# Casts, weight loads, late q rows and the order of the first layer-1 units in a fused attention and MLP kernel

## The chip, the core and the metric

The kernel runs on one core of a Trainium2 chip. The metric is the device time of one execution in microseconds (us), the median of three runs. The engines are TensorE (PE; its weight loads are listed as PEld), VectorE (DVE), ScalarE (ACT), GpSimd (POOL) and SyncE (SP, which here only issues transfers). Transfers issued by SyncE run in the hardware queue q1, those issued by GpSimd in the software queue q0; 16 DMA engines serve both.

## What is computed

Eight batches of eight heads, 576 rows and 64 columns. q is softmaxed over its columns, k over the sequence; kv = kᵀv for each head, and the head's output is q times kv. The heads' outputs side by side are x, 4608 rows by 512, and a two-layer MLP follows with a leaky ReLU between its layers.

```python
def _attn_ref(q, k, v):
    q_s = exp(q - max(q, axis=-1));  q_s = q_s / sum(q_s, axis=-1)
    k_s = exp(k - max(k, axis=2));   k_s = k_s / sum(k_s, axis=2)
    kv = einsum('bhsd,bhse->bhde', k_s, v)
    return einsum('bhsd,bhde->bhse', q_s, kv)

def _moe_ref(x, w_in, w_out):        # 512 x 2048 and 2048 x 512
    h = x @ w_in
    return maximum(0.01 * h, h) @ w_out
```

## The kernel before

**Tiles.** A batch's q, k and v are loaded as tiles of 128 partitions by 4 by 9 by 64: partitions hold two heads' 64 row groups, the 4 is a pair of heads (`HL`), and the 9 (`R`) are sequence rows. Rows are taken in groups: `RA` is rows 0 to 3, `R1` rows 4 and 5, `R2` rows 6 to 8. Head pairs 0 and 1 of a tile (`H0`) and 2 and 3 (`H1`) are also called group `gg` 0 and 1. The MLP works in nine blocks of 512 rows of x (`TT`); block 0 needs most of batch 0, block t most of batch t. x is kept transposed in `xT`, four channel blocks `cb` 0 to 3 by 4608 columns.

**A unit of layer 1** is a pair of output blocks j, j+1 of 128 channels of the 2048. In block 0 the 512 columns are done in two halves of 256. `layer1` (L455) accumulates the four channel blocks in the order 0, 2, 1, 3 into `ph`, a bank of PSUM; `leaky` (L464, ScalarE) evacuates it to `gj`. After half one and half two, 8 units each, `layer2` (L476) accumulates into `pout`: for each j of 16 four matmuls of 512 columns, with `w_out` row block j.

**Before block 0** the code is written out by hand, and each engine runs its own instructions in the order of that text. k's maximum over the sequence goes through TensorE and VectorE (`k_tree` L162, `k_max_pe`, `k_all_dve`, `k_all_pe`), VectorE subtracts it (`k_sub_ps`, L364), ScalarE exponentiates (`k_exp`, L203) and casts v to bf16 with a column of ones behind it (`v_cast`, L213 on ScalarE, L215 elsewhere). `kv_pair` (L293) makes kᵀv and the sums for a group, `kd_rec` and `kd_one` (L375, L379) divide by the sums. q's rows 0 to 3 are exponentiated row by row with their sums (`q_first`, L239), divided (`q_first_rec` L251, `q_norm` L280), transposed on TensorE (`q_transpose`, L392) and copied to `qT` (`q_keep`, L407 on ScalarE, L409 on VectorE). `attend` (L415) multiplies kd with qT and copies the result to `xT` (L425 ScalarE, L427 VectorE). `wake(n)` (L326) puts n dummy matmuls of 512 columns on TensorE. Block 0 starts with four units of half one on channel blocks 0 and 2 only; then `attend` of blocks 1 and 3; then these units are ended with channel blocks 1 and 3.

**Late rows and the next batch** are hung into block 0 by `at(t, u, ...)`: the functions run behind unit step u of block t (half one is 0 to 15, half two 16 to 31, layer 2's j is 32 to 47). `q_max` (L226), `q_sub` (L256), `q_exp` (L264), `q_sum` (L273, L275) and `q_norm` treat R1 and R2; batch 1's k and q preparation hangs on step 15, its exponentials and casts on 29 to 33, its kv on 41, its attends on 46 and 47.

**Loads.** `load` (L79) issues q, k and v on SyncE. `load_w_in(fh)` (L133) issues half fh of w_in (1024 of 2048 output channels) on GpSimd as four transfers, each a quarter: `gg` 0 (channel blocks 0 and 2) in two, `gg` 1 (blocks 1 and 3) in two. `load_w_out(js)` (L140) issues row blocks js. Both cast from f32 to bf16 on the way. A copy of one element into `gate` on GpSimd makes the issues behind it wait: half 0 of w_in for batch 0's k (L513), half 1 for k's subtraction (L539), w_out for the first half of batch 1's k (L569). `hold_sync` (L508) is a small transfer that makes SyncE's later loads wait: batch 1's loads for the first quarter of w_in's half 1, batch 2's for w_out's block 11.

Of the kernel before, what the change touches and what calls it, by code (L numbers as in the profile page):

```python
# [8 lines left out]
FP32 = mybir.dt.float32  # L9
BF16 = mybir.dt.bfloat16  # L10
AF = mybir.ActivationFunctionType
ALU = mybir.AluOpType
# [13 lines left out]
def kernel(  # L26
# [60 lines left out]
    R1, R2 = slice(4, 6), slice(6, R)  # L87
# [38 lines left out]
    w_in_r = moe_w_in.rearrange("(gg hp hh d) f -> gg hp d hh f", gg=2, hp=2, hh=2)  # L126
    w_in_t = w_in_sb.rearrange("p (hh gg) f -> p gg hh f", gg=2)
# [100 lines left out]
    def q_first(b, rs):  # L228
# [3 lines left out]
        qsum = small_pool.tile([P, n, HL], FP32, name="qsum")  # L232
        for hs in (slice(0, 2), slice(2, 4)):
# [3 lines left out]
            for h in range(hs.start, hs.stop):  # L237
                for r in range(n):
                    nc.scalar.activation(  # L239
                        out=st[b]["qe"][:, rs.start + r, h],  # L240
                        in_=st[b]["q"][:, h, rs.start + r],
                        func=AF.Exp,
                        bias=nmax[:, h, r : r + 1],
                        accum_out=qsum[:, r, h : h + 1],
                    )
        st[b]["qsum"] = qsum

    def q_first_rec(b, rs):
        n = rs.stop - rs.start
        st[b]["qrec", rs.start] = qrec = small_pool.tile([P, n, HL], FP32, name="qrec")  # L250
        nc.vector.reciprocal(out=qrec, in_=st[b]["qsum"])  # L251
# [25 lines left out]
    def q_norm(b, rs):  # L277
        n = rs.stop - rs.start
        qes = st[b]["qe"][:, rs]
        nc.vector.tensor_tensor(  # L280
# [245 lines left out]
    k_tree(0, H1, slice(1, 4))  # L526
    k_max_pe(0, 1)
# [17 lines left out]
    wake(4)  # L545
    q_transpose(0, 0, 4)
    kv_pair(0, 1)
    for hh in range(2):
        kd_rec(0, 0, hh)
        kd_one(nc.vector, 0, 0, hh)  # L550
    q_keep(nc.scalar, 0, 0, 4, slice(0, 4, 2))
    q_keep(nc.vector, 0, 0, 4, slice(1, 4, 2))
    attend(0, [0, 2], 0, 256, nc.scalar)
    wake(3)
    kd_rec(0, 1, 0)
    kd_rec(0, 1, 1)
    kd_one(nc.vector, 0, 1, 0)
    kd_one(nc.vector, 0, 1, 1)
    q_max(0, R1)
    q_sub(nc.gpsimd, 0, R1)  # L560
    q_max(0, R2)
# [7 lines left out]
    nc.gpsimd.tensor_copy(out=gate[:, 0:1], in_=st[1]["k"][:, 0, 0, 0:1])  # L569
    for j0, j1 in ((0, 2), (2, 4), (4, 8), (8, 12), (12, 16)):  # L570
        load_w_out(slice(j0, j1))
    hold_sync(1, w_out_sb[0:1, 11, 0:128])
    load_all(2)
# [4 lines left out]
    at(0, 11, lambda: q_transpose(0, 4, 2), lambda: q_keep(nc.vector, 0, 4, 2))  # L578
    at(0, 13, lambda: q_transpose(0, 6, 3), lambda: q_keep(nc.vector, 0, 6, 3))
    at(0, 15, lambda: attend(0, [0, 2], 256, 256, nc.scalar))  # L580
    at(0, 15, lambda: attend(0, [1, 3], 256, 256, nc.vector))
    at(0, 17, lambda: attend(0, [0, 1, 2, 3], 512, 64, nc.scalar))
    at(0, 15, lambda: k_begin(1), lambda: q_begin(1), lambda: k_tree(1, H0), lambda: k_tree(1, H1))
    at(0, 15, lambda: k_allmax(1), lambda: k_sub(nc.gpsimd, 1, H0), lambda: k_sub(nc.vector, 1, H1))
    at(0, 15, lambda: q_max(1, RA), lambda: q_sub(nc.gpsimd, 1, RA))
    at(0, 15, lambda: q_max(1, RB), lambda: q_sub(nc.gpsimd, 1, RB))
# [3 lines left out]
    at(0, 33, lambda: v_cast(nc.scalar, 1, 1), lambda: q_exp(1, RB), lambda: q_sum(1, RB))  # L590
# [58 lines left out]
    begun = []  # L649
    for j in range(0, 8, 2):  # L650
        ph = psB_pool.tile([P, 2, 256], FP32, name="ph", tag=BANK_TAG)
        for i in range(2):
            layer1(j + i, ph[:, i], 0, 256, slice(0, 2), i == 0)
        begun.append(ph)
    attend(0, [1, 3], 0, 256, nc.scalar)
    for half in range(2):
        for j in range(0, NF, 2):
            part = slice(2, 4) if begun else slice(0, 4)
            ph = begun.pop(0) if begun else psB_pool.tile([P, 2, 256], FP32, name="ph", tag=BANK_TAG)
            for i in range(2):  # L660
                layer1(j + i, ph[:, i], 256 * half, 256, part, i == 0, i == 1)
                if i == 1:
                    leaky(g_sb[j // 2][:, :, 256 * half : 256 * half + 256], ph)
                run(0, 16 * half + j + i)
# [65 lines left out]
```

## Time and profile before

| | |
|---|---|
| median of three runs | 289.98 us (289.98 to 290.32) |
| profiled execution, its own time | 290.49 us |
| its span, first to last instruction | 288.7 us |
| TensorE busy | 278.3 us, 96% of the span |
| VectorE, ScalarE, GpSimd busy | 146.9, 149.5, 85.5 us |
| granted TensorE clock | 1.000 |
| dummy matmuls (L326) | 30, 9.7 us |
| layer 1 of block 0, first matmul to the start of layer 2 | 17.00 to 35.75 us |
| layer 1 of block 1 begins | 52.98 us |

The profiled execution is one run under the hardware profiler; its own time is 0.51 us above the median. Times in the profile count from the span's start. A busy TensorE is not one at its peak. The landing of a transfer is given as the time from its issue until all of it has arrived.

Landings (issue, time to landing) that matter here: w_in's half 0 in four quarters issued from 7.90 to 9.85 landed after 5.8 to 7.8 us; half 1, issued from 13.03 to 14.8, landed after 6.8 to 8.6 us; w_out's five pieces, issued from 25.32 to 28.26, after 9.2, 10.8, 12.7, 14.5 and 16.3 us; batch 1's k in two halves, issued at 20.53 and 21.14, after 4.2 and 5.7 us, q, issued at 21.72, after 8.3 us, and v, issued at 22.40, after 14.2 us.

### The profile page before, as it was taken

Reading aid. Unit: us, or ns where it says so; the run is one execution under the profiler, and the core shown is the slowest. Engines: PE = TensorE matmul, PEld = TensorE weight load, DVE = VectorE, ACT = ScalarE, POOL = GpSimd, SP = SyncE. Lnnn points to the kernel's source line nnn. Section 1 sums busy time; section 2 is a strip of 40 time slices with the busy share of each in tenths; the row PEclk is TensorE's granted clock in tenths of the full one; section 3 lists DMA queues with packets and bytes.
Section 4 is the critical chain, followed back from the end, with each engine's and each line's share of the span. In section 5 each row is a group of like instructions: output and inputs, shape, how many; then the busy total and the mean of one; then the engine's idle time right before and its main releaser. Section 6 shows DMA issues by size and latency. Waiting matters only on the chain.

```text
span 288.7 us, 4880 instructions
## 1 busy us (share of the span) xinstructions
PE 278.3 (96%) x1960; PEld 137.4 (48%) x1960; DVE 146.9 (51%) x244; ACT 149.5 (52%) x268; POOL 85.5 (30%) x61
## 2 busy tenths in 40 slices
PE   8686999999999999999999999999999999999995
PEld 3265845444444445444444544554445444444443
DVE  2947957896890696199276636654531200110011
ACT  4956684569068506942684349433853066016400
POOL 4545280008039207703910491039100000000000
PEclk9999999999999999999999999999999999999999
DMA  7999999787549454964299139923131310131033
GB/s 251 320 205 346 268 177 336 229 254 313 104 109 346 163 118 108 357 180 111 66 347 241 39 80 327 265 48 75 36 84 36 73 36 3 38 82 26 2 72 73
DMA packets 36582, 45.79 MB, mean 159 GB/s; under 512 B 15952, under 2 KB 19280, under 8 KB 36560
## 3 DMA queue, kind: packets, MB, share of 16 engines
q1 hardware_dynamic: 33120, 41.16, 48.5%
q0 software_dynamic: 3280, 4.20, 8.4%
q8 instruction: 15, 0.25, 0.3%
q10 hardware_dynamic: 160, 0.13, 0.1%
q14 instruction: 7, 0.06, 0.1%
HBM read 36.70 MB, written 9.44 MB: 160 GB/s over the span
## 4 chain that ended last, share of the span: by engine, by line
PE 85%; DMA 10%; POOL 2%; issue 1%; SPq 1%; ACT 0%; DVE 0%; POOLq 0%
PE pout L476 42%; PE ph L455 38%; DMA w_out_sb<-in_moe_w_out_dram 4%; DMA k_raw<-in_k_dram 4%; DMA w_in_sb<-in_moe_w_in_dram 2%; PE po L443 2%; PE pkv L293 2%; POOL w_in_sb L133 1%; POOL w_out_sb L140 1%; PE psum_qt L392 0%; SPq L79 0%; PE po L415 0%; SPq L508 0%; ACT xT L425 0%; DVE out_sb L470 0%
## 5 line engine op out<-in xcount | busy, mean ns | idle before, releaser
L476 PE MATMUL pout<-w_out_sb,gj 128*128 128x512 bf16 (+2 forms) x592 | 130.5, 373 | 0.1
L455 PE MATMUL ph<-xT,w_in_sb 128*128 128x512 bf16 (+1 forms) x640 | 127.5, 358 | 3.1 <-DMA w_in_sb<-in_moe_w_in_dram 1.6
L464 ACT ACTIVATE gj<-ph 128x512 bf16<-128x512 f32 x144 | 82.4, 603 | 56.7 <-PE ph L455 56.1
L455 PEld LDWEIGHTS <-w_in_sb 128*128 128x128 bf16 x640 | 62.1, 98 | 65.0 <-issue 4.6
L476 PEld LDWEIGHTS <-gj 128*128 128x128 bf16 x592 | 57.0, 98 | 62.3 <-issue 0.4
L470 DVE COPY out_sb<-pout 128x512 f32<-128x512 f32 (+1 forms) x34 | 22.7, 674 | 85.7 <-PE pout L476 80.1
L195 POOL TENSOR_TENSOR k_raw<-k_raw,kall 128x2304 f32<-128x2304 f32 (+1 forms) x6 | 29.1, 4846 | 81.2 <-DVE kall L187 68.6
L273 DVE TENSOR_REDUCE qsum<-qe 128x36 f32<-128x2304 bf16 (+4 forms) x11 | 19.8, 1798 | 37.4 <-ACT qe L264 37.4
L256 POOL TENSOR_TENSOR q_raw<-q_raw,qmax 128x2304 f32<-128x2304 f32 (+4 forms) x11 | 31.1, 2840 | 25.1 <-DVE qmax L226 25.1
L449 ACT CAST xT<-po 128x320 bf16<-128x320 f32 (+1 forms) x48 | 16.8, 402 | 40.0 <-PE po L443 40.0
L203 ACT ACTIVATE ke<-k_raw 128x2304 bf16<-128x2304 f32 (+2 forms) x11 | 17.5, 1597 | 10.6 <-POOL k_raw L195 8.9
L280 DVE TENSOR_TENSOR qe<-qe,qrec 128x2304 bf16<-128x2304 bf16 (+4 forms) x12 | 21.7, 1811 | 0.4
L226 DVE TENSOR_REDUCE qmax<-q_raw 128x36 f32<-128x2304 f32 (+4 forms) x11 | 19.4, 1788 | 0.0
L264 ACT ACTIVATE qe<-q_raw 128x2304 bf16<-128x2304 f32 (+4 forms) x11 | 16.9, 1533 | 0.8 <-POOL q_raw L256 0.8
L215 POOL CAST vb<-v_raw 128x1152 bf16<-128x1152 f32 x12 | 13.5, 1153 | 0.0
L326 PE MATMUL pout<-zero 128*128 128x512 bf16 x30 | 9.7, 461 | 1.3 <-POOL zero L101 1.3
L162 DVE TENSOR_TENSOR t<-k_raw 128x1024 f32<-128x1024 f32 (+1 forms) x10 | 10.1, 1011 | 0.4
L162 DVE TENSOR_TENSOR t<-t 128x256 f32<-128x256 f32 (+2 forms) x20 | 9.6, 478 | 0.7
L443 PE MATMUL po<-qX,kd 128*128 128x320 bf16 (+1 forms) x48 | 9.8, 286 | 0.0
L470 ACT COPY out_sb<-pout 128x512 f32<-128x512 f32 (+1 forms) x3 | 1.7, 564 | 14.9 <-PE pout L476 14.9
L315 DVE TENSOR_TENSOR kd<-pkv,krec 64x128 bf16<-64x128 f32 x28 | 8.1, 289 | 0.7
L293 PEld LDWEIGHTS <-ke 64*64 64x64 bf16 x576 | 5.5, 106 | 4.7 <-ACT gj L464 1.7
(55 smaller groups left out, 100.7 us busy)
## 6 DMA issues: line engine op xcount, KB each, us to landing
out_dram<-out_sb SPq DMA_DIRECT2D x70, 128.0 KB, 2.4
q_raw<-in_q_dram SPq DMA_DIRECT2D x7, 1152.0 KB, 8.1
v_raw<-in_v_dram SPq DMA_DIRECT2D x7, 1152.0 KB, 11.2
k_raw<-in_k_dram SPq DMA_DIRECT2D x6, 1152.0 KB, 5.8
k_raw<-in_k_dram SPq DMA_DIRECT2D x4, 576.0 KB, 5.4
w_in_sb<-in_moe_w_in_dram POOLq DMA_DIRECT2D x8, 256.0 KB, 7.1
w_out_sb<-in_moe_w_out_dram POOLq DMA_DIRECT2D x3, 512.0 KB, 14.5
v_raw<-in_v_dram SPq DMA_DIRECT2D x2, 576.0 KB, 7.4
```

Of the source, the lines that this page charges most:

```text
L162: nc.vector.tensor_tensor(out=o, in0=i0, in1=i1, op=ALU.max)
L195: eng.tensor_tensor(out=ks, in0=ks, in1=st[b]["kall"][:, hs].unsqueeze(2).to_broadcast([P, n, R, D]), op=ALU.subtract,)
L203: nc.scalar.activation(out=st[b]["ke"][:, :, hs].rearrange("p r h d -> p h r d"), in_=st[b]["k"][:, hs], func=AF.Exp,)
L226: nc.vector.tensor_reduce(out=m, in_=st[b]["q"][:, :, rs], axis=AX.X, op=ALU.max)
L256: eng.tensor_tensor(out=qs, in0=qs, in1=st[b]["qmax", rs.start].unsqueeze(3).to_broadcast([P, HL, n, D]), op=ALU.subtract,)
L264: nc.scalar.activation(out=st[b]["qe"][:, rs].rearrange("p r h d -> p h r d"), in_=st[b]["q"][:, :, rs], func=AF.Exp,)
L273: nc.vector.reduce_sum(out=qsum, in_=st[b]["qe"][:, rs], axis=AX.X)
L280: nc.vector.tensor_tensor(out=qes, in0=qes, in1=st[b]["qrec", rs.start].unsqueeze(3).to_broadcast([P, n, HL, D]), op=ALU.mult,)
L455: nc.tensor.matmul(ph, lhsT=w_in_sb[:, cb, j * P : (j + 1) * P], rhs=xT[:, cb, c0 : c0 + n], start=(i == 0 and first), stop=(i == NB - 1 a ...
L464: nc.scalar.activation(out=o, in_=ph, func=AF.Prelu, alpha=LEAKY_SLOPE)
L470: copy(out=out_sb, in_=pout)
L476: nc.tensor.matmul(pout, lhsT=g_sb[j // 2][:, j % 2, tsub * P : (tsub + 1) * P], rhs=w_out_sb[:, j, os], start=(j == 0), stop=(j == NF - 1),)
```

## The change

Batch 0's rows get a third late group: R2 becomes rows 6 and 7, and R3 is row 8.

1. v's first group is cast on GpSimd instead of ScalarE, behind a gate on k's maximum. ScalarE keeps the second group.
2. The first four rows of q are kept by group: sums, reciprocals, normalise, transposes and copy each for one group (`qsum2`, `qrec2`, `q_first_norm`, `q_turn_first`, `q_keep_first`). Group 0 is normalised on GpSimd, group 1 on VectorE; qT of group 0 is copied by VectorE, of group 1 by ScalarE.
3. `load_w_in(1)` is issued behind GpSimd's normalise, with no gate of its own. w_out's first piece (row blocks 0 and 1) is issued behind GpSimd's subtraction of R1; the others, now (2,4), (4,6), (6,8), (8,12), (12,16), behind a gate on w_in's last element, inside block 0's step 0.
4. The attends of the first 256 columns are done one channel block at a time: 0 and 2 before the second `kv_pair`, 1 and 3 between the first units' channel blocks.
5. Block 0's order of units: four units of half one on channel blocks 0 and 2, ended with 1 and 3; then the other four units of half one begun on channel blocks 0 and 2, with the transposes of rows 4 to 7 and the attends of columns 256 to 511 in between; then four unit steps (j 0 to 3) of half two; then the end of the begun four; then the rest of half two.
6. R1 is exponentiated in the gap before the fourth attend and normalised on GpSimd; R3's steps lie in the gaps of item 5. Batch 1's preparation moves from step 15 to 20, its exponentials and first cast from 29 to 33 to 31 and 32, with the cast behind both k exponentials.
7. Six dummy matmuls fewer: `wake(5)` becomes 3, `wake(4)` becomes 3, and the last `wake(3)` is gone.

```diff
+    nc.gpsimd.tensor_copy(out=gate[:, 0:1], in_=st[0]["kmax"][:, HL - 1, D - 1 : D])
+    v_cast(nc.gpsimd, 0, 0)
     k_max_pe(0, 1)
...
-    wake(5)
+    wake(3)
+    q_first_rec(0, 0)
+    q_first_norm(nc.gpsimd, 0, 0)
+    load_w_in(1)
     k_sub_ps(0, 0, HB)
     k_exp(0, slice(1, 2))
-    v_cast(nc.scalar, 0, 0)
     v_cast(nc.scalar, 0, 1)
+    q_first_rec(0, 1)
     k_sub_ps(0, 1)
-    nc.gpsimd.tensor_copy(out=gate[:, 0:1], in_=st[0]["k"][:, HL - 1, R - 1, D - 1 : D])
-    load_w_in(1)
     k_exp(0, H1)
-    q_first_rec(0, RA)
-    q_norm(0, RA)
     kv_pair(0, 0)
-    wake(4)
-    q_transpose(0, 0, 4)
+    q_turn_first(0, 0)
+    wake(3)
+    kd_rec(0, 0, 0)
+    kd_one(nc.vector, 0, 0, 0)
+    q_keep_first(nc.vector, 0, 0)
+    kd_rec(0, 0, 1)
+    kd_one(nc.vector, 0, 0, 1)
+    q_first_norm(nc.vector, 0, 1)
+    attend(0, [0], 0, 256, nc.scalar)
+    attend(0, [2], 0, 256, nc.scalar)
     kv_pair(0, 1)
...
+    q_turn_first(0, 1)
+    q_keep_first(nc.scalar, 0, 1)
     q_max(0, R1)
     q_sub(nc.gpsimd, 0, R1)
+    load_w_out(slice(0, 2))
...
-    nc.gpsimd.tensor_copy(out=gate[:, 0:1], in_=st[1]["k"][:, 0, 0, 0:1])
-    for j0, j1 in ((0, 2), (2, 4), (4, 8), (8, 12), (12, 16)):
-        load_w_out(slice(j0, j1))
...
+    def behind_first_units():
+        q_max(0, R3)
+        q_sub(nc.gpsimd, 0, R3)
+        nc.gpsimd.tensor_copy(out=gate[:, 0:1], in_=w_in_sb[:, NB - 1, F - 1 : F])
+        for j0, j1 in ((2, 4), (4, 6), (6, 8), (8, 12), (12, 16)):
+            load_w_out(slice(j0, j1))
+        hold_sync(1, w_out_sb[0:1, 11, 0:128])
+        load_all(2)
...
-    at(0, 3, lambda: q_exp(0, R1), lambda: q_sum(0, R1), lambda: q_norm(0, R1))
-    at(0, 5, lambda: q_exp(0, R2), lambda: q_sum(0, R2), lambda: q_norm(0, R2))
...
+    at(0, 0, lambda: q_sum(0, R1), lambda: q_norm(0, R1, nc.gpsimd), behind_first_units)
+    at(0, 2, lambda: q_exp(0, R2), lambda: q_sum(0, R2), lambda: q_norm(0, R2))
+    at(0, 22, lambda: q_transpose(0, 8, 1), lambda: q_keep(nc.scalar, 0, 8, 1))
+    at(0, 26, lambda: attend(0, [0, 1, 2, 3], 512, 64, nc.scalar))
+    at(0, 20, lambda: k_begin(1), lambda: q_begin(1), lambda: k_tree(1, H0), lambda: k_tree(1, H1))
+    at(0, 20, lambda: k_allmax(1), lambda: k_sub(nc.vector, 1, H1), lambda: k_sub(nc.gpsimd, 1, H0))
...
-    at(0, 29, lambda: k_exp(1, H1))
-    at(0, 31, lambda: v_cast(nc.scalar, 1, 0), lambda: k_exp(1, H0))
-    at(0, 33, lambda: q_exp(1, RA), lambda: q_sum(1, RA), lambda: q_norm(1, RA))
+    at(0, 31, lambda: k_exp(1, H1), lambda: k_exp(1, H0), lambda: v_cast(nc.scalar, 1, 0))
+    at(0, 32, lambda: q_exp(1, RA), lambda: q_sum(1, RA), lambda: q_norm(1, RA))
...
+    def begin(js, parts):
+        phs = [psB_pool.tile([P, 2, 256], FP32, name="ph", tag=BANK_TAG) for _ in js]
+        for i, between in parts:
+            for j, ph in zip(js, phs):
+                for h in range(2):
+                    layer1(j + h, ph[:, h], 0, 256, slice(i, i + 1), h == 0, False)
+            for fn in between:
+                fn()
+        return phs
...
+    t1 = (lambda: q_transpose(0, 4, 2), lambda: q_keep(nc.scalar, 0, 4, 2), lambda: q_exp(0, R3))
+    t2 = (lambda: q_transpose(0, 6, 2), lambda: q_keep(nc.vector, 0, 6, 2), lambda: q_sum(0, R3))
+    x2 = (
+        lambda: attend(0, [0, 2], 256, 256, nc.scalar),
+        lambda: attend(0, [1, 3], 256, 256, nc.vector),
+        lambda: q_norm(0, R3),
+    )
+    x1 = (lambda: attend(0, [1], 0, 256, nc.scalar),)
+    x3 = (lambda: q_exp(0, R1), lambda: attend(0, [3], 0, 256, nc.scalar))
...
+    J0, J1 = range(0, 8, 2), range(8, NF, 2)
+    for j, ph in zip(J0, begin(J0, ((0, x1), (1, x3)))):
+        end(j, ph, 0, slice(2, 4), False)
+    begun = begin(J1, ((0, t1), (1, t2 + x2)))
+    for j in (0, 2):
+        whole(j)
+    for j, ph in zip(J1, begun):
+        end(j, ph, 0, slice(2, 4), False)
+    for j in range(4, NF, 2):
+        whole(j)
```

`end` finishes a unit, evacuates it with `leaky` and runs the hooks of its two steps; `whole(j)` does a unit of half two in one piece.

More of the change, by code (lines that the diff above doesn't have):

```diff
@@ L86 @@
     RA, RB = slice(0, 4), slice(4, R)
-    R1, R2 = slice(4, 6), slice(6, R)
+    R1, R2, R3 = slice(4, 6), slice(6, 8), slice(8, R)
     st = [{} for _ in range(B)]
@@ L231, in q_first @@
         st[b]["nmax"] = nmax = small_pool.tile([P, HL, n], FP32, name="nmax")
-        qsum = small_pool.tile([P, n, HL], FP32, name="qsum")
-        for hs in (slice(0, 2), slice(2, 4)):
+        for gg in range(2):
+            hs = slice(2 * gg, 2 * gg + 2)
+            st[b]["qsum", gg] = qsum = small_pool.tile([P, n, 2], FP32, name="qsum2")
             nc.vector.tensor_reduce(
@@ L275, in q_sum, with q_norm @@
         nc.vector.reciprocal(out=qrec, in_=qsum)
-    def q_norm(b, rs):
+    def q_norm(b, rs, eng=nc.vector):
         n = rs.stop - rs.start
         qes = st[b]["qe"][:, rs]
-        nc.vector.tensor_tensor(
+        eng.tensor_tensor(
             out=qes,
@@ L648 @@
     g_sb = g_tiles()
[L649 to L664, printed above, removed]
+    def begin(js, parts):
+        phs = [psB_pool.tile([P, 2, 256], FP32, name="ph", tag=BANK_TAG) for _ in js]
+        for i, between in parts:
+            for j, ph in zip(js, phs):
+                for h in range(2):
+                    layer1(j + h, ph[:, h], 0, 256, slice(i, i + 1), h == 0, False)
+            for fn in between:
+                fn()
+        return phs
@@ new lines, in end @@
+    def end(j, ph, half, part, first):
+        for h in range(2):
+            layer1(j + h, ph[:, h], 256 * half, 256, part, first and h == 0, h == 1)
+            if h == 1:
+                leaky(g_sb[j // 2][:, :, 256 * half : 256 * half + 256], ph)
+            run(0, 16 * half + j + h)
+    t1 = (lambda: q_transpose(0, 4, 2), lambda: q_keep(nc.scalar, 0, 4, 2), lambda: q_exp(0, R3))
[4 more added lines that the diff above has]
+        lambda: q_norm(0, R3),
+    )
@@ new lines, with whole @@
+    x1 = (lambda: attend(0, [1], 0, 256, nc.scalar),)
+    x3 = (lambda: q_exp(0, R1), lambda: attend(0, [3], 0, 256, nc.scalar))
+    def whole(j):
+        end(j, psB_pool.tile([P, 2, 256], FP32, name="ph", tag=BANK_TAG), 1, slice(0, 4), True)
+    J0, J1 = range(0, 8, 2), range(8, NF, 2)
[6 more added lines that the diff above has]
+        end(j, ph, 0, slice(2, 4), False)
```

70 lines of the change are left out of this document (38 added, 32 removed).

## The prediction

> **What bounds the kernel now.** I read the shares first, then the chain that ended last, then TensorE's timeline up to the first layer-2 matmuls, and last the transfers. TensorE is busy 278.3 of 288.7 us and the granted clock is full in every slice. The chain from 52.98 us on, where block 1 begins (64 matmuls of 512 columns, L455), is matmuls without a gap to the end. The change touches only what lies before that, so its worth is by how much that start moves.
>
> ```profile
> 24.86 0.18 POOL gate L569
> ...
> 26.78 12.70 DMA w_out_sb<-in_moe_w_out_dram
> ...
> 39.52 5.34 PE pout L476 x24
> ...
> 52.98 13.97 PE ph L455 x64
> ```
>
> In the chain (start, us, what) the reader sees a DMA in front of block 0's layer 2: a piece of w_out is awaited until 39.48. In TensorE's timeline (start, us, line, count, idle before and its releaser) layer 1 of block 0 runs from 17.00 to 35.75, with waits for xT twice and for w_in once:
>
> ```profile
> 13.37 0.48 PE L293 MATMUL pkv<-vb,ke 64*64 64x65 bf16 x36 [0.80 <-ACT vb L213]
> ...
> 17.00 1.91 PE L455 MATMUL ph<-xT,w_in_sb 128*128 128x256 bf16 x16
> ...
> 19.80 2.12 PE L455 MATMUL ph<-xT,w_in_sb 128*128 128x256 bf16 x18 [0.67 <-ACT xT L425]
> 23.50 1.69 PE L455 MATMUL ph<-xT,w_in_sb 128*128 128x256 bf16 x14 [1.57 <-DMA w_in_sb<-in_moe_w_in_dram]
> ...
> 28.65 1.03 PE L455 MATMUL ph<-xT,w_in_sb 128*128 128x256 bf16 x8 [0.72 <-ACT xT L425]
> ...
> 35.75 9.10 PE L476 MATMUL pout<-w_out_sb,gj 128*128 128x512 bf16 x40
> ```
>
> The DMA view, asked for windows of one us (queue: packets, MB, share), shows what the loads of batch 1 (q1) and of the weights (q0) do to each other. From 28 to 29 us and from 31 to 32 us:
>
> ```profile
> q1 hardware_dynamic: 173, 0.37, 103.5%
> ```
> ```profile
> q1 hardware_dynamic: 83, 0.19, 56.7%
> q0 software_dynamic: 82, 0.08, 54.4%
> ```
>
> Alone the batch loads move 173 packets a us. Beside w_out they move 83, one for one with it.
>
> **Front part.** Removed from ScalarE: the cast of v's first pair (1.14 us) ahead of the last k exponential. GpSimd takes it: free of w_in's issues at 10.47, a gate copy, 1.15 us (its own casts, L215) to 11.8, then one q normalise of 512 elements, bounded by its row of 512 f32 elements, 1.04 us, and twice that; I take 1.04, since it has the same two inputs: done 12.8. VectorE gets a second reciprocal, 0.24 us, in front of each of two k subtractions. So ke's second head is ready at 12.5 and the first kv pair starts at 12.6 (13.37 before). The last k exponential starts at 13.6 (14.27), the second pair at 14.8 (15.48). VectorE's first kd and qT copy are done by 14.15 and its half normalise (0.69, the 512 row) by 15.2. The second four transposes follow at 15.25, and layer 1 starts at **15.5** (17.00): six dummy matmuls are gone (1.3 us) and it needs only xT blocks 0 and 2.
>
> Its first 16 matmuls (0.109 us each) and attends 1 and 3 end at 17.9. ScalarE's copy of block 3 waits behind the first late exponential (0.63), so TensorE idles 0.65 to 18.55, and the first four units end at 20.2 (21.55 before). The next four need w_in's second half: its first two quarters landed at 19.84 and 20.8, and ScalarE frees the last bank at about 21.7. Then 16 matmuls with the transposes of rows 4 to 7 between them, until 23.0. Now comes a new exposed wait: transposes, copy to qT (0.42), attends (0.60) and copies to xT (0.59 and 0.69) in series, two us of which TensorE fills 0.66: **1.4 us idle** that lay under other matmuls before (there 0.72 showed). Removed against it: the 1.57 us wait for w_in. From 25.0, 80 matmuls at 0.109, two transposes and four small attends, 9.2 us: layer 2 starts at **34.2** instead of 35.75. Bounds 33.6 (copies 0.3 shorter on each leg) and 35.2 (a bank or a late row costs another us).
>
> On GpSimd's own queue w_in's four issues (2.4 us in all) end at 15.2, the subtraction of rows 4 and 5 at 16.9, w_out's first issue (0.75) at 17.6, that of rows 6 and 7 at 18.65; ScalarE wants it at 19.5, so the issue moved past it costs nothing with 0.85 of cover, and its whole 0.75 without. SyncE's queue keeps its order: the wait on w_in, batch 1's loads, the wait on w_out, batch 2's loads (wanted at 55.9, landed 6 us after the wait).
>
> Late q rows on GpSimd (0.69 of VectorE's work becomes about 1.04) end at 20.1 and are wanted at 22: free; if that cover were gone it would cost its whole 1.04. The last row and batch 1's preparation come after hook 20 instead of 15; VectorE reaches batch 1's first k maximum at 25.4 (28.57 before), so nothing is later there: its subtractions on GpSimd end at 40.0 instead of 42.56.
>
> **If nothing else bound**, block 1 would start at 34.2 + 17.1 (35.75 to 52.98 less the 0.15 wait) = 51.3, a gain of 1.7. Two transfers stand in between.
>
> **w_out.** The piece for units 8 to 11 landed at 42.0 (27.5 plus 14.5) and was used at about 43.1, so at unchanged landing the gain is at most 1.0. All engines are at full rate from 2 to 42 us; moving an issue makes no bandwidth. Only earlier work of w_in moves it: the first half's quarters land 1.3 apart, 17.6 the last, but the next one at 19.84, 2.2 later, so some engine ran dry for about 0.9. That half was issued at 13.03 to 15.4, beside VectorE's normalise of 1,024 elements (13.04 to 14.27); now it is issued from 12.8, beside subtractions from PSUM and a half normalise. Between 0.2 (the issue alone) and 1.2 (the dry stretch too) earlier; I take 1.0.
>
> [...]
>
> **v of batch 1, the new wait.** w_out's first piece is now queued right behind w_in, and the rest follows a gate on w_in's end (23.47) instead of k's first pair (24.73, gate copy 24.86, issue 25.32): issue at 23.6, 1.7 earlier. Both run against k, q, v of batch 1. By landings of the last engine before: 64 of its 96 packets until 30.0 alone, about 0.105 us each; the last 32 beside w_out in 6.6 us, 0.206 each. The first piece has 256 packets, 16 an engine: 16 pairs take 3.3 us, in which the batch would have moved 31: 15 behind. The earlier start of the rest costs 1.7 us at half rate: 8 more. 23 packets at 0.206 = 4.7 us. v landed at
>
> ```profile
> v_raw<-in_v_dram SPq DMA_DIRECT2D x1, 1152.0 KB, 14.2
> ```
>
> that is 22.40 + 14.2 = 36.6; now 36.6 + 4.7 - 1.0 (w_in sooner) - 0.4 (DMA engines 10 to 27% idle between 21.5 and 22.5, which the queued piece fills) = **39.9**, bounds 36.6 (no change) and 43 (4.7 once more for slower engines, less 1.0 and the rest).
>
> On ScalarE the cast of v (hook 31) now stands ahead of q's exponentials, and all wait. From landing V: cast 1.07, exponential 1.06, sum 1.25, reciprocal 0.29, normalise, sum 1.5, reciprocal, normalise 1.49: V + 8.25 for the last rows' transposes; then 0.55, two units 1.73, attends 0.49, a unit 0.86, attends and copy 0.77: block 1 starts at V + 12.65. Before this was 49.25, hidden; now 52.55 against 52.98. **Sum: 0.43, with rounding a gain of 0.5 us**: 290.49 of the profiled execution becomes 290.0, and the median, 0.51 lower (289.98), **289.5**.
>
> **Rivals.** (1) v is not late (w_out starts as slowly as in 29 to 30 us, 31 packets against 136): V under 39, and the front and w_out decide, gain 1.2 to 1.7, **288.5**. For: first contacts were slow twice. Against: the first piece has waited in the queue for five us. (2) v later still, the other sign: at 41 to 43 us with w_in landing no sooner; block 1 starts at 53.65 to 55.65, **291.6** in the middle; it decides from V = 40.3 on and loses over 0.6 from 40.9. For: the packets go one for one and the last engine is 1 us behind. Against: w_in ending sooner counts fully for v, and the 1 us counted for it is not the most that its rows allow. (3) The thinner stretch from 12 to 18 us loses clock: 32 matmuls at twice 0.109 add 3.5 us, **293**; against it, the clock stayed 1.00 over 1.57 us of idle, and the longest gap I find is 1.4. The Trainium skill, "TensorE: Matmul & The Clock Gate", Part 1, halves the clock after an idle window of about 3.4 us; no run here shows one. (4) That the edit does nothing: excluded by the order it writes.
>
> **Chances.** Forecast 0.45 (288.7 to 290.4), rival 1 0.20, rival 2 0.30, rival 3 0.05. A measurement of this kernel can tell 0.2%, 0.58 us. Faster: rival 1 and 0.22 of the forecast's, 0.42. Within: the forecast's other 0.23. Slower: 0.35. Range 288.3 (rival 1's far end) to 291.9, which leaves out the clock and the tail of rival 2.
>
> **What would show it.** First layer-1 matmul near 15.5, an idle of about 1.4 before the ninth unit group near 25, layer 2 from 34.2; v of batch 1 landing near 39.9 with ScalarE idle before its cast and TensorE waiting for the transposes of batch 1. If v lands by 38, rival 1; if block 1 starts after 53.6, rival 2. It is wrong if the front gains under 0.5 or the loads do not share one for one.

## The result and the profile after

| | before | after |
|---|---|---|
| median | 289.98 us (289.91 to 290.32, 5 runs) | 289.00 us (288.79 to 289.12, 5 runs) |
| ratio after : before | | 0.9961 [0.9946, 0.9976] |
| profiled execution, its own time | 290.49 us | 288.90 us |
| its span | 288.7 us | 287.1 us |
| first layer-1 matmul of block 0 | 17.00 us | 15.00 us |
| layer 2 of block 0 begins | 35.75 us | 33.85 us |
| v of batch 1 landed | 36.6 us | 37.9 us |
| block 1 begins | 52.98 us | 51.38 us |

The change is 1.0 us (0.39%) faster by the medians and 1.6 us by the two profiled executions. About 0.25 us of the latter is not the change: k's first transposed maximum, which waits for nothing that was edited, starts at 7.92 us here and at 8.17 in the profile of before; the rest is that the profiled execution of before lies 0.5 us above its median. From block 1's start to the end of the span both kernels take 235.7 us, so the start of block 1 tells the whole difference, as the prediction assumed.

TensorE's timeline of the changed kernel (start, us, line, count, idle before and what ended it):

```profile
15.00 1.10 PE L485 MATMUL ph<-xT,w_in_sb 128*128 128x256 bf16 x8
...
17.52 1.93 PE L485 MATMUL ph<-xT,w_in_sb 128*128 128x256 bf16 x16 [0.32 <-DMA w_in_sb<-in_moe_w_in_dram]
20.85 1.03 PE L485 MATMUL ph<-xT,w_in_sb 128*128 128x256 bf16 x8 [1.39 <-DMA w_in_sb<-in_moe_w_in_dram]
...
23.72 0.61 PE L445 MATMUL po<-qT,kd 128*128 128x256 bf16 x4 [0.52 <-DVE qT L439]
24.79 5.07 PE L485 MATMUL ph<-xT,w_in_sb 128*128 128x256 bf16 x44 [0.46 <-ACT xT L455]
...
33.85 8.80 PE L506 MATMUL pout<-w_out_sb,gj 128*128 128x512 bf16 x39
...
46.97 0.72 PE L422 MATMUL psum_qt<-ident,qe 128*128 128x128 bf16 x10 [0.44 <-DVE kd L345]
...
51.38 3.83 PE L485 MATMUL ph<-xT,w_in_sb 128*128 128x512 bf16 x16
```

Layer 1 starts two us sooner, but then waits for w_in twice. The longer wait ends at 20.85, when the second quarter of w_in's half 1 is there; before, the units that came here needed all four quarters and went on at 23.50. Two short waits follow (for qT and for xT), then nothing stops TensorE until the wait for kd at 46.97. The idle time in brackets counts from the end of the matmul's record before it. Records overlap by 0.16 us (in layer 2 each is 0.38 long, and one starts every 0.22), so a wait costs 0.16 more than is listed, and a short one is not listed at all: the 0.44 at 46.97 cost 0.61 us.

The chain that ended last (start, us, what) no longer goes through w_out:

```profile
22.14 15.74 DMA v_raw<-in_v_dram
...
38.96 1.06 ACT qe L294
40.05 1.23 DVE qsum L303
41.66 1.23 DVE qe L310
42.88 1.41 DVE qsum L303
44.62 1.49 DVE qe L310
```

It is the landing of batch 1's v, and behind it ScalarE's and VectorE's work on q for the last rows of batch 1. ScalarE's timeline shows why q waits for v, which it does not use: the cast stands first in ScalarE's order.

```profile
37.90 1.15 ACT L214 CAST vb<-v_raw 128x1152 bf16<-128x1152 f32 x1 [0.87 <-DMA v_raw<-in_v_dram]
38.96 1.05 ACT L294 ACTIVATE qe<-q_raw 128x1024 bf16<-128x1024 f32 x1
```

The transfers in windows of one us (queue: packets, MB, share); the changed kernel from 22 to 23 us, from 25 to 26, and from 28 to 29:

```profile
q0 software_dynamic: 177, 0.18, 106.0%
q1 hardware_dynamic: 43, 0.06, 15.8%
...
q1 hardware_dynamic: 194, 0.41, 104.9%
...
q1 hardware_dynamic: 88, 0.20, 58.3%
q0 software_dynamic: 92, 0.09, 55.2%
```

The kernel before, from 22 to 23 us:

```profile
q1 hardware_dynamic: 107, 0.22, 76.8%
q0 software_dynamic: 12, 0.02, 9.2%
```

w_out's first piece went through mostly between 21 and 23 us, ahead of the batch loads: their first packet came at 22.7 us, and at 21.5 in the kernel before, though k was issued at 20.5 in both. The rest of w_out was issued from 23.81 us on, but no packet of it came before 27.8; until then the batch loads had the engines almost to themselves. From 28 us on the two queues shared one for one.

### The profile page after: what moved, and what is told of

It reads as the page before. It is cut to its first block, busy times and chain, and to the rows that moved or that the text cites. A ratio compares the mean times of both kernels' runs of the same rounds, so it can differ in the third digit from the quotient of the medians.

```text
span 287.1 us, 4854 instructions
## 1 busy us (share of the span) xinstructions
PE 275.8 (96%) x1927; PEld 136.4 (48%) x1954; DVE 145.7 (51%) x247; ACT 149.4 (52%) x272; POOL 89.6 (31%) x66
## 4 chain that ended last, share of the span: by engine, by line
PE 82%; DMA 10%; DVE 2%; POOL 1%; issue 1%; SPq 1%; ACT 1%; DVEq 0%; ACTq 0%
PE pout L506 39%; PE ph L485 38%; DMA v_raw<-in_v_dram 5%; DMA w_in_sb<-in_moe_w_in_dram 3%; PE po L473 2%; DMA k_raw<-in_k_dram 2%; PE pkv L323 2%; DVE qe L310 1%; DVE qsum L303 1%; SPq L79 1%; POOL w_in_sb L134 1%; POOL vb L216 0%; ACT qe L294 0%; PE psum_qt L422 0%; SPq L538 0%
## 5 line engine op out<-in xcount | busy, mean ns | idle before, releaser
L500 DVE COPY out_sb<-pout 128x512 f32<-128x512 f32 (+1 forms) x34 | 22.7, 676 | 85.7 <-PE pout L506 80.0
L310 DVE TENSOR_TENSOR qe<-qe,qrec 128x2304 bf16<-128x2304 bf16 (+4 forms) x11 | 19.9, 1809 | 0.3
L216 POOL CAST vb<-v_raw 128x1152 bf16<-128x1152 f32 x13 | 14.6, 1151 | 0.0
L356 PE MATMUL pout<-zero 128*128 128x512 bf16 x23 | 7.5, 462 | 1.4 <-POOL zero L101 1.3
L345 DVE TENSOR_TENSOR kd<-pkv,krec 64x128 bf16<-64x128 f32 x28 | 8.1, 288 | 0.7
```

What stands on the lines that cost most here:

```text
L310: eng.tensor_tensor(out=qes, in0=qes, in1=st[b]["qrec", rs.start].unsqueeze(3).to_broadcast([P, n, HL, D]), op=ALU.mult,)
L500: copy(out=out_sb, in_=pout)
```

## The experiments

All times are of the profiled execution of each kernel unless a median is named. T is the start of block 0's layer 2; J1 is the matmul behind the wait for the second quarter of w_in's half 1 (20.85 above); V is the landing of batch 1's v; B is the start of block 1. The span less B lies between 235.6 and 235.9 us in every kernel here, so B is read for the size of an effect, and the ratio for whether a measurement resolves it. Each ratio is against runs of before on the same chip, whose medians were 290.25 us for e1 to e4, 290.10 for e5 to e8 and 290.22 for e9 to e11. Beside e1 to e8 some runs of before had a lowered clock (last section), which puts those ratios up to 0.002 under the quotient of the medians.

| kernel | J1 | T | V | B | median us | ratio |
|---|---|---|---|---|---|---|
| before | | 35.75 | 36.6 | 52.98 | 289.98 | 1 |
| change | 20.85 | 33.85 | 37.9 | 51.38 | 289.00 | 0.9961 [0.9946, 0.9976] |
| e1 | 20.67 | 33.80 | 34.3 | 50.72 | 288.56 | 0.9933 [0.9908, 0.9958] |
| e2 | | 35.99 | 38.7 | 53.17 | 290.19 | 0.9995 [0.9973, 1.0018] |
| e3 | 20.61 | 33.62 | 37.7 | 50.54 | 288.49 | 0.9924 [0.9895, 0.9953] |
| e4 | 20.72 | 33.72 | 36.5 | 50.74 | 288.58 | 0.9924 [0.9893, 0.9954] |
| e5 (change again) | 20.56 | 33.56 | 37.8 | 51.29 | 288.87 | 0.9942 [0.9920, 0.9964] |
| e6 | 21.08 | 34.03 | 38.6 | 51.24 | 288.42 | 0.9933 [0.9907, 0.9959] |
| e7 | 21.02 | 34.02 | 38.1 | 50.94 | 288.76 | 0.9940 [0.9919, 0.9961] |
| e8 | 20.73 | 33.27 | 35.1 | 50.75 | 288.81 | 0.9945 [0.9925, 0.9965] |
| e9 | 20.84 | 33.15 | 37.9 | 50.34 | 287.91 | 0.9918 [0.9905, 0.9931] |
| e10 | 20.65 | 37.05 | 37.7 | 54.41 | 292.45 | 1.0073 [1.0049, 1.0097] |
| e11 | 21.03 | 33.26 | 38.2 | 50.48 | 287.78 | 0.9916 [0.9903, 0.9929] |

B less T is 16.92 us in e1, e3 and e7, where TensorE waits for nothing between T and B. What a kernel has above that is a wait, and the starts of its matmuls show which: 0.31 in before (for the piece of w_out that ended at 39.48), 0.61 in the change (for kd, behind v's chain), 0.27 in e2 (for kd), 0.10 in e4 (for w_out), 0.30 in e6 (in kv, for v's second cast), 0.56 in e8 (for w_out), 0.44 in e10 (in kv), and in e9 and e11 0.2 for w_out and about 0.1 in kv.

### e1: w_out behind batch 1's k, as before

```diff
     q_sub(nc.gpsimd, 0, R1)
-    load_w_out(slice(0, 2))
...
-        nc.gpsimd.tensor_copy(out=gate[:, 0:1], in_=w_in_sb[:, NB - 1, F - 1 : F])
-        for j0, j1 in ((2, 4), (4, 6), (6, 8), (8, 12), (12, 16)):
+        nc.gpsimd.tensor_copy(out=gate[:, 0:1], in_=st[1]["k"][:, 0, 0, 0:1])
+        for j0, j1 in ((0, 2), (2, 4), (4, 6), (6, 8), (8, 12), (12, 16)):
```

> The changed kernel with w_out's issues put back behind the first half of batch 1's k (no early first piece, the gate as before; the six pieces stay). Theory A (the early issue of w_out pays, because layer 2 now starts at 33.85 and would wait for it): batch 1's v lands near 36.6 again, the piece for units 8 to 11 near 42.0, TensorE waits for w_out about 1 us, block 1 starts near 51.9; 0.5 us slower than the changed kernel, 289.5. Rival B (the early issue only delays v, and v decides): block 1 starts near 50.9, 0.4 us faster, 288.6.

v landed at 34.3 us instead of 37.9, and from T to B it took 16.92 us instead of 17.53. From T on no matmul waited for w_out, although its piece for units 8 to 11 landed at 40.1, and none for kd. T stayed where it was but for 0.1 us (T less J1 is 13.13 instead of 13.00, as w_out's first piece landed only at 33.76), so GpSimd's issue in front of the subtraction of rows 6 and 7 had indeed cost nothing. By the two profiles the earlier issue of w_out gained 0.1 us at most and cost 0.6 us through v. Three of the twelve runs of e1 took 289.53 to 290.65 us, against 288.12 to 288.95 for the others; what held them up is not shown.

### e2: the kernel before with w_out issued as in the change

```diff
     q_sub(nc.gpsimd, 0, R1)
+    load_w_out(slice(0, 2))
...
-    nc.gpsimd.tensor_copy(out=gate[:, 0:1], in_=st[1]["k"][:, 0, 0, 0:1])
-    for j0, j1 in ((0, 2), (2, 4), (4, 8), (8, 12), (12, 16)):
+    nc.gpsimd.tensor_copy(out=gate[:, 0:1], in_=w_in_sb[:, NB - 1, F - 1 : F])
+    for j0, j1 in ((2, 4), (4, 6), (6, 8), (8, 12), (12, 16)):
```

> The kernel before with nothing but w_out's issues moved as in the change. Theory A (the first piece fills DMA time that stood idle, the rest delays v to about 37.9, which is still hidden here): layer 2 starts at 35.75 with no wait for w_out, block 1 near 52.8, 289.8. Rival B (the prediction's charge, one packet of the batch lost for each of w_out's, v at 39.9 or later): v's cast, which stands before k's second exponential here, makes block 1 start near 54.4, 1.4 us slower, 291.4.

The time did not change by more than its interval. v landed 2.1 us later than in the kernel before, and ScalarE's timeline shows that its cast did wait:

```profile
38.71 1.15 ACT L213 CAST vb<-v_raw 128x1152 bf16<-128x1152 f32 x1 [0.90 <-DMA v_raw<-in_v_dram]
```

But TensorE reached layer 2 only at 35.99, so most of the delay stayed covered: block 1 began at 53.17, not at the 54.4 that the prediction's sums give. B less T is 17.18 here and 17.23 before, and that these are nearly equal is chance: the wait of 0.31 for w_out is gone, and one of 0.27 for kd, behind v's chain, has come. A v as late as this costs 0.3 in a kernel whose front ends at 36 us, and one 0.8 us sooner costs 0.6 where the front ends at 33.8.

### e3: v's casts behind q's exponentials

```diff
-    at(0, 31, lambda: k_exp(1, H1), lambda: k_exp(1, H0), lambda: v_cast(nc.scalar, 1, 0))
+    at(0, 31, lambda: k_exp(1, H1), lambda: k_exp(1, H0))
     at(0, 32, lambda: q_exp(1, RA), lambda: q_sum(1, RA), lambda: q_norm(1, RA))
-    at(0, 32, lambda: v_cast(nc.scalar, 1, 1), lambda: q_exp(1, RB), lambda: q_sum(1, RB))
+    at(0, 32, lambda: v_cast(nc.scalar, 1, 0), lambda: q_exp(1, RB), lambda: q_sum(1, RB), lambda: v_cast(nc.scalar, 1, 1))
```

> The changed kernel with ScalarE's order for batch 1 altered: q's first exponential, v's first cast, q's second exponential, v's second cast. Theory A (the landing of v at 37.9 and the chain behind it set block 1's start): the wait of 0.44 for the transposes of batch 1's last rows goes, block 1 starts near 50.95, 0.45 us faster than the changed kernel, 288.5. Rival B (TensorE's own work and w_out set it): no change, 289.0.

v landed as late as in the change (37.7 us), yet B less T fell to 16.92 us, the value of e1. ScalarE's timeline of e3:

```profile
37.51 1.06 ACT L294 ACTIVATE qe<-q_raw 128x1024 bf16<-128x1024 f32 x1 [0.70 <-POOL q_raw L286]
38.47 1.14 ACT L214 CAST vb<-v_raw 128x1152 bf16<-128x1152 f32 x1
```

q's exponential now starts at 37.51 instead of 38.96, and the cast finds v there. So what the late v cost came through ScalarE's order, and not through kv, which needs the cast and was in time. e1 and e3 remove the same 0.6 us, from two sides.

### e4: w_out's first piece with the others

```diff
     q_sub(nc.gpsimd, 0, R1)
-    load_w_out(slice(0, 2))
...
-        for j0, j1 in ((2, 4), (4, 6), (6, 8), (8, 12), (12, 16)):
+        for j0, j1 in ((0, 2), (2, 4), (4, 6), (6, 8), (8, 12), (12, 16)):
```

> The changed kernel with w_out's first piece issued with the others, behind the gate on w_in's end. Theory A (that piece fills DMA time that stood idle from 21.5 to 23): v lands within 0.4 us of 37.9, w_out ends some 0.5 us later, time within 0.3 us of 289.0. Rival B (the prediction: the piece costs v 3.1 us): v lands near 34.8, the chain behind v no longer binds, 0.4 us faster.

v landed at 36.5 us, 1.4 sooner than in the change: between what the two theories said (B had 34.8). It was enough to free the chain, as B said: B less T is 17.02, and the 0.10 above 16.92 is a wait for w_out's piece for units 8 to 11, which landed at 40.69. The batch loads' first packet came at 21.4 us, 1.3 sooner than in the change, which is about the 1.4. The other 2.2 us, from 36.5 to the 34.3 of e1, belong to the earlier start of the remaining pieces, as far as one profile of each can tell.

### e5: the change again

> The changed kernel once more, on the chip of the next three. If the chain behind v sets block 1's start, that start lies 17.5 us behind layer 2's start as before, not the 16.9 of the kernels in which the chain was shortened; ratio to the kernel before near 0.996, against 0.993 for those.

The ratio is 0.9942 [0.9920, 0.9964] on a second chip. B less T is 17.7 us, with a wait of 0.64 for kd. The first quarter of w_in's half 1 was there at 18.66 us; it was 19.82 in the first profile of the same kernel, and over these runs it lies between 18.66 and 20.22. So a difference of one us in this landing between two kernels shows nothing, and nothing here shows that the early piece of w_out delays it. Nor does v follow it: the batch loads wait for this landing and were issued 1.2 us sooner than in the first profile, but their first packet came at 22.6 us again, and v at 37.8.

### e6: the begun units ended first, then half two in one piece

```diff
-    begun = begin(J1, ((0, t1), (1, t2 + x2)))
-    for j in (0, 2):
-        whole(j)
+    begun = begin(J1, ((0, t1), (1, t2)))
     for j, ph in zip(J1, begun):
         end(j, ph, 0, slice(2, 4), False)
-    for j in range(4, NF, 2):
+    for fn in x2:
+        fn()
+    for j in range(0, NF, 2):
         whole(j)
```

This and the next three kernels have e3's edit as well.

> The kernel with the casts behind q's exponentials (e3), and the four unit steps of half two taken out from between the halves of the begun units: the begun units are ended first, then come the attends of columns 256 to 511, then all of half two. Theory A (what counts is that the begun units use w_in's first two quarters; the wait for w_in's last quarters, some 0.4, and the copies' 0.6 are about what the units of half two save): layer 2 starts within 0.2 us of e3's 33.6, time within 0.3 of e3. Rival B (the four steps of half two are what gained the time in the front): layer 2 starts 0.8 us later or more, time 0.8 us above e3.

T less J1 is 12.95 us, against 13.0 in e3 and in the change: without the four unit steps of half two in the middle nothing is lost. A wait of 0.15 for w_in and one of 0.88 for xT stand where 0.52 and 0.46 stood. So those steps are worth nothing that can be measured. B less T is 17.21 here, as kv stood still until v's second cast ended at 43.32.

### e7: v's first cast of batch 0 back on ScalarE

```diff
     nc.gpsimd.tensor_copy(out=gate[:, 0:1], in_=st[0]["kmax"][:, HL - 1, D - 1 : D])
-    v_cast(nc.gpsimd, 0, 0)
...
     k_exp(0, slice(1, 2))
+    v_cast(nc.scalar, 0, 0)
     v_cast(nc.scalar, 0, 1)
```

> The kernel with the casts behind q's exponentials (e3), and the first cast of v of batch 0 back on ScalarE. Theory A (an earlier first layer-1 matmul is lost again in the wait for w_in's second half at 20.6): first layer-1 matmul near 16.2 instead of 15.3, layer 2 within 0.2 us of 33.6, time as e3. Rival B (the prediction's sum, in which each us of the front counts but for what w_in's landing takes): layer 2 0.6 to 0.9 us later, time 0.6 to 0.9 above e3.

The first layer-1 matmul starts at 15.89 us, 0.9 after that of the change, but TensorE then waits only 0.59 for w_in, where it waited 1.39, and T less J1 is 13.0 again. J1 and with it T are 0.4 later than in e3, by the landing of w_in, which varies more than that from run to run. The intervals of e3, e5 and e7 overlap: the cast on GpSimd moves the start and not measurably the time; up to 0.3 us cannot be excluded.

### e8: e3, e1 and the transposes earlier

```diff
-    begun = begin(J1, ((0, t1), (1, t2 + x2)))
+    begun = begin(J1, ((0, t1 + t2), (1, x2)))
```

The transposes of rows 6 and 7 go one channel block earlier, so that their copy to qT is covered by matmuls; e1's and e3's edits are in it too.

> The changed kernel with the casts behind q's exponentials (e3), w_out's issue behind batch 1's k (e1), and the transposes of rows 6 and 7 one channel block earlier, so that their copy to qT lies under eight matmuls. Theory A (front's exposed wait of 0.52 goes, nothing else binds): layer 2 starts near 33.1, block 1 near 50.0, 0.5 us below e3, 288.0. Rival B (w_out, issued late, now binds): layer 2 near 33.1, a wait of some 0.5 for the piece of units 8 to 11, time as e3.

T less J1 fell to 12.5 us, as meant; the last 0.2 to the 12.3 of e9 below were lost to w_out's first piece, which landed at 33.23. And now layer 2 outran w_out; TensorE's timeline:

```profile
33.27 1.89 PE L506 MATMUL pout<-w_out_sb,gj 128*128 128x512 bf16 x7
35.55 7.07 PE L506 MATMUL pout<-w_out_sb,gj 128*128 128x512 bf16 x32 [0.39 <-DMA w_out_sb<-in_moe_w_out_dram]
```

The second piece is late for a layer 2 that starts at 33.27 us, by 0.56 as the starts count it. The gain is given back: B is 50.75, later than with e3 alone. It was the rival here that was right. Its twelve runs fall into two groups of six, 287.72 to 288.46 us and 289.17 to 289.64, and the median lies between them; the profile is one of the faster group, and what the slower group lost is not shown.

### e9: e3 and the transposes earlier, w_out as in the change

> The kernel with the casts behind q's exponentials (e3), w_out's issues as in the change, and the transposes of rows 6 and 7 one channel block earlier. Theory A (with w_out early nothing binds but TensorE's front): layer 2 starts 12.5 us behind the start of the second four units instead of 13.0, block 1 16.9 behind that, 0.5 us below e3, 288.0. Rival B (another transfer binds, w_out's second piece or v): a wait behind layer 2's start, time as e3's 288.5.

```profile
20.84 1.03 PE L485 MATMUL ph<-xT,w_in_sb 128*128 128x256 bf16 x8 [1.09 <-DMA w_in_sb<-in_moe_w_in_dram]
21.71 0.61 PE L422 MATMUL psum_qt<-ident,qe 128*128 128x128 bf16 x8
...
24.09 5.07 PE L485 MATMUL ph<-xT,w_in_sb 128*128 128x256 bf16 x44 [0.46 <-ACT xT L455]
...
33.15 9.01 PE L506 MATMUL pout<-w_out_sb,gj 128*128 128x512 bf16 x40
```

In TensorE's timeline of e9 the eight transposes come together and the wait of 0.52 for qT is gone; layer 2 begins 12.3 us after J1, with w_out's first pieces there. The ratio to before is 0.9918 [0.9905, 0.9931]: faster than before, and below the interval of the change's first measurement (that of e5 overlaps it by 0.001). So an early w_out is worth something once the front is short enough to outrun it, if v's cast is no longer in q's way. B less T is 17.19 and not 16.92, and that is mostly w_out again: the piece for units 8 to 11 landed at 40.23 us, and the timeline of TensorE's weight loads has a step just there.

```profile
38.98 0.96 PEld L506 LDWEIGHTS <-gj 128*128 128x128 bf16 x5
40.28 1.39 PEld L506 LDWEIGHTS <-gj 128*128 128x128 bf16 x7 [0.34 <-issue]
```

Matmuls start 0.22 us apart up to 39.84, and the next one starts at 40.28: 0.22 lost. Somewhat under 0.1 more is lost in kv, whose second half follows v's second cast (to 42.42). In the change the same piece landed at 40.01 and was wanted at 40.76, so it had 0.75 us to spare.

### e10: the second four units one by one

```diff
-    begun = begin(J1, ((0, t1), (1, t2 + x2)))
-    for j in (0, 2):
-        whole(j)
-    for j, ph in zip(J1, begun):
-        end(j, ph, 0, slice(2, 4), False)
-    for j in range(4, NF, 2):
+    for j, fns in zip(J1, ((), t1, t2, x2)):
+        end(j, psB_pool.tile([P, 2, 256], FP32, name="ph", tag=BANK_TAG), 0, slice(0, 4), True)
+        for fn in fns:
+            fn()
+    for j in range(0, NF, 2):
         whole(j)
```

With e3's edit. Each unit takes all four channel blocks before the next begins, as in the kernel before; the start of layer 1 stays as early as in the change.

> The kernel with the casts behind q's exponentials (e3), and the second four units of half one done one by one with all four channel blocks, as in the kernel before, the late transposes and attends behind the second, third and fourth of them, half two in one piece. Theory A (beginning these units on the channel blocks of w_in's first two quarters is what gained the front): TensorE stands still after two matmuls until w_in's last quarter at 23.4, layer 2 starts near 35.5, time 1.8 us above e3, 290.3, as the kernel before. Rival B (the earlier start and the late rows gained it): layer 2 within 0.5 us of e3's 33.6, time within 0.5 of 288.5.

```profile
20.65 0.38 PE L485 MATMUL ph<-xT,w_in_sb 128*128 128x256 bf16 x2 [1.26 <-DMA w_in_sb<-in_moe_w_in_dram]
23.14 2.73 PE L485 MATMUL ph<-xT,w_in_sb 128*128 128x256 bf16 x14 [2.11 <-DMA w_in_sb<-in_moe_w_in_dram]
...
26.09 1.50 PE L485 MATMUL ph<-xT,w_in_sb 128*128 128x256 bf16 x8
```

In TensorE's timeline the matmuls go on at 23.14 us, where the kernel before went on at 23.50. It is slower than before by 0.73%, and that is more than the order can give: eight matmuls that take 1.04 us elsewhere took 1.50 at 26.09. The table of windows (window, its length, then busy us of PE, PEld, DVE, ACT and POOL, the granted clock, DMA share, GB/s) tells why:

```profile
20.15:23.55 3.40, 0.79 (x6) 0.53 (x7) 0.73 (x2) 0.54 (x2) 0.18 (x1) 1.00 1.15 244
23.55:27.00 3.45, 3.45 (x21) 2.58 (x20) 0.00 (x0) 1.69 (x4) 3.39 (x5) 0.51 1.05 408
```

After a stretch in which TensorE was busy 0.79 of 3.40 us, the clock was halved for 3.45. The mean clock of this execution is 0.994, and 0.006 of 290.2 us is 1.74 us. Its nine runs have mean clocks from 0.988 to 0.998; each time less its own loss, so worked out, has a median of 290.1 us, against 290.22 for before. This working is an estimate, since a lowered mean clock need not cost its share: three runs of e7 at 0.993 took 288.71 to 288.93 us, no longer than its others. But the two runs of e10 at 0.998, 290.53 and 290.75, lie near it. So two things are in this result: the order of the units is worth 1.6 us (290.1 less e3's 288.49), which is all that the change gains and its lost 0.6 besides, and the clock takes 2.3 on top. A layer 1 that starts two us earlier is by itself worth next to nothing (290.1 against 290.22).

### e11: the attends inside the second channel block

```diff
-    begun = begin(J1, ((0, t1 + t2), (1, x2)))
+    begun = begin(J1, ((0, t1 + t2), (1, ())), x2)
```

It is e9 with the attends of columns 256 to 511 behind the second unit of the second channel block, instead of behind the fourth.

> e9 with the attends of columns 256 to 511 put behind the first two units of the second channel block, so that the other two units cover their copies to xT. Theory A (the copies' 0.45 go under four matmuls): layer 2 starts 12.2 us behind the start of the second four units, time 0.3 us below e9, 287.7. Rival B (the attends now wait for the copies to qT and the gap only moves): 12.5 us, time as e9.

```profile
22.35 0.60 PE L485 MATMUL ph<-xT,w_in_sb 128*128 128x256 bf16 x4
23.03 0.61 PE L445 MATMUL po<-qT,kd 128*128 128x256 bf16 x4
23.48 5.79 PE L485 MATMUL ph<-xT,w_in_sb 128*128 128x256 bf16 x48
```

In TensorE's timeline the wait for xT is no longer shown. But layer 2 began 12.2 us after J1, where e9 had 12.3: a part of the idle time now lies in front of the attends. Layer 2 then waited 0.2 for w_out's piece for units 8 to 11, as in e9 (landed at 40.34, next matmul at 40.38), so less of a gain in the front could come through. The ratio, 0.9916 [0.9903, 0.9929], is the lowest measured and not to be told from that of e9.

## Why the prediction was right, and where it was off

The forecast was a gain of 0.5 us, and the medians show 1.0. Its mechanism is the one measured: the front gains under two us, and a v of batch 1 that lands later takes a part of it back. Two sizes in it were wrong, with opposite signs: v's landing by 2.0 us and the chain behind it by 0.85. That the time came out within 0.5 us is in part luck. With v's true landing alone the sum would have left the front to decide, at 51.3 (rival 1); with the true chain alone it would have put block 1 at 53.4, a loss. In the two profiles block 1 began 1.6 us sooner, where 0.43 was forecast.

**The front.** Layer 1 was to start at 15.5 us (15.00 measured, 0.25 of it ahead before the change acts), and layer 2 at 34.2 (33.85). The steps between were less exact than their sum. The first four units ended at 19.45, not 20.2, since ScalarE's copy of block 3 was not late and only 0.32 us of waiting showed. The next units waited for w_in until 20.85, not for a bank until 21.7. The new wait, put at 1.4 us, came as 0.52 and 0.46. From there to layer 2 it took 9.06 us, where 9.2 was worked out. What the text did not say is which edit the gain hangs on: e7 and e10 show that it is not the casts and the earlier start but the order of the second four units, which needs two quarters of w_in at 20.85 and the other two only after 24.8. The 17.1 us from layer 2 to block 1 should have been 16.92: the wait for w_out in the kernel before, read as 0.15, is 0.31 by the starts.

**w_in sooner by 1.0 us: not shown.** The issues did move, from 13.03 to 12.40. The first quarter of half 1 landed at 19.80 us (19.84 before), and the copy that waits for the last one ran at 23.35 (the prediction had 23.47 for its end before). So no run shows the gain counted for taking the issues away from VectorE's normalise; the landings moved by 0.0 to 0.2 us. With a spread of 1.5 us between runs in the first quarter's landing, no run excludes a gain of that size either.

**w_out as a cap of 1.0: not in force.** The piece for units 8 to 11 landed at 40.0 us instead of 42.0 and nothing waited for it; e1 shows that even 40.1 was in time, and, as w_out is issued there as before, that its earlier issue is not what moved it. The cap was 0.75 us away: with layer 2 at 33.15 to 33.26 this piece costs 0.2 (e9, e11), and with w_out issued late the first two pieces cost more (e8).

**v at 39.9 us: the term that was too large.** It landed at 37.9. The sum had 3.1 us for the first piece, 1.7 for the earlier start of the rest, less 1.0 and 0.4. e4 measures the first piece at 1.4: it did not run packet for packet against the batch loads but held them off until it was nearly through, so that their first packet came 1.2 us later. In the nine profiles with the early piece that packet came at 22.6 to 22.9 us, and in the four without at 21.4 to 21.6, whenever k was issued (19.3 to 20.9). Here the sign that the prediction named for being wrong, loads that do not share one for one, did show (177 and 43 packets from 22 to 23 us); later both queues moved the same number (88 and 92). Why the first piece went ahead is open. The rest of w_out had its first packet 1.6 us sooner (27.8 against 29.4), as counted, and cost 2.2 by e4 and e1. The base moved too: in e1 and e8, which issue w_out as before, v landed at 34.3 and 35.1 us, not at 36.6. From 25 to 28 us the batch loads moved 163 to 166 packets a us in the kernel before and 178 to 187 in e8; why is not shown.

**V + 12.65 us to block 1: the term that was too small.** It was 13.5 (37.88 to 51.38). The chain left out that VectorE makes batch 1's kd between the last normalise and the last transposes: two reciprocals and two pairs of multiplications, from 46.03 to 47.6, the first pair of which the transposes at 46.97 waited for.

```profile
44.62 1.49 DVE L310 TENSOR_TENSOR qe<-qe,qrec 128x1280 bf16<-128x1280 bf16 x1
46.03 0.17 DVE L342 RECIPROCAL krec<-pkv 128x2 f32<-128x2 f32 x1
46.23 0.59 DVE L345 TENSOR_TENSOR kd<-pkv,krec 64x128 bf16<-64x128 f32 x2
```

In VectorE's timeline of the changed kernel the normalise ends at 46.1 and kd comes right behind it; the releaser of the transposes is L345. With v 2.0 us too late and the chain 0.85 too short, the forecast for block 1 was 52.55, and it began at 51.38.

**The rivals.** Rival 1 (288.5 us) had its condition met, v under 39 us, and its sign too, v by 38, but its consequence not: v's chain still decided, as the forecast said, and e1 and e3 show its price, 0.6 us. The result lies between the two. Rival 2 needed v at 40.3 or later. Rival 3, the clock, did not occur in the changed kernel, and did in e10, where the waits are longer.

**What stays open.** The steps of late rows on GpSimd and the fewer dummy matmuls were not tried alone. The times of e1, e3 and e4 lie 0.4 to 0.5 us below the change, but their intervals overlap with it; that v's chain costs 0.6 rests on B less T, which is 17.5 and 17.7 in two profiles of the change, and 16.9 to 17.0 in those three. The order of units is shown by one kernel, e10, whose time has to be freed of the clock's loss by an estimate.

## What to carry to other kernels

When weights still arrive, order the work so that it needs the pieces in the order in which they land; an earlier start in front of a late piece only makes the wait longer. On an engine that works in order, an instruction that waits for a transfer belongs behind the work that is ready: here one cast in front of an exponential turned a transfer of little urgency into the chain that decided. Before a transfer is issued earlier, ask what it shares the engines with; the same earlier issue of w_out was neutral (e2, where it put one wait in the place of another), a loss (the change against e1) and needed (e9 against e8, by their profiles), by how early the front ended. When a wait is removed, look for the next one by the starts of the matmuls: some were too short for the timeline to list, and w_out was waited for again in the two fastest kernels.

## What the hardware showed unexpectedly

- **The clock fell after waits that were broken by work.** In e10 the idle stretches were 1.26 and 2.11 us, with two matmuls between them, and the clock was halved for 3.4 us behind them. The Trainium skill, "TensorE: Matmul & The Clock Gate", Part 1, has a free-running window of 3413 ns and a halved clock after an idle one: the 3.4 us of half speed agree with its length, but the 3.40 us before them were not idle (0.79 us busy). The loss comes in such units: 51 runs of before beside e1 to e8 hold 8 with a mean clock of 0.994, which took 291.9 to 292.4 us, while the others took 289.75 to 290.97. A run of e2 at 0.993 took 292.69, but three of e7 at 0.993 took no longer than its others, so a lowered mean clock does not always cost time. No run of the change itself (16) had one.
- **A queue of issued transfers is not yet traffic.** In the change the first packet of w_out's gated pieces came 4.0 us after their issue at 23.81 (at 27.8), and in the kernel before 4.1 us after that at 25.32 (at 29.4); in the other eleven profiles it was 4.0 to 4.1 us too. For that time the other queue had all engines.
- **Landings of the same transfer vary by more than most edits are worth.** The first quarter of w_in's half 1 was there between 18.66 and 20.22 us in profiles of kernels that issue it alike. The second quarter, for which TensorE waits, let it go on at 20.56 to 21.08, and T follows that one.
